# One table for the order of every engine's single steps, in block-causal attention followed by a gated MLP

## The chip, the core and the metric

The kernel runs on one core of one Trainium2 chip. The core has five engines with a queue of instructions each: TensorE (PE, matrix products into PSUM), VectorE (DVE), ScalarE (ACT), GpSimd (POOL) and SyncE (SP, which here only issues DMA transfers). Every engine works through its own queue in order, and engines wait for each other by semaphores. The metric is the device time of one execution in microseconds (us); three runs of the kernel before gave 657.11, 653.99 and 655.95, a median of 655.95.

## What is computed

Eight batches of eight heads, 576 positions, head size 64. The attention's output is the input of a gated MLP with a spatial mix. All inputs are float32.

```python
def _attn_ref(q, k, v):
    block = 64
    scores = scale * np.matmul(q, k.transpose(0, 1, 3, 2))
    mask = block_i >= block_j
    scores = np.where(mask, scores, -1000000000.0)
    scores = scores - np.max(scores, axis=-1, keepdims=True)
    attn = np.exp(scores)
    attn = attn / (np.sum(attn, axis=-1, keepdims=True) + 1e-09)
    return np.matmul(attn, v).astype(np.float32)

def _moe_ref(x, w_in, w_spatial, b_spatial, w_out):
    h = np.maximum(x @ w_in, 0.0)
    u, v = (h[..., :d_ff // 2], h[..., d_ff // 2:])
    v_n = (v - mu) / np.sqrt(var + 1e-06)
    v_s = np.einsum('ts,bsd->btd', w_spatial, v_n) + b_spatial[None, :, None]
    gated = u * v_s
    return (gated @ w_out).astype(np.float32)
```

Here x is the attention's output with the heads side by side (576 x 512), w_in is 512 x 1024, w_spatial 576 x 576, w_out 512 x 512; mu and var are the mean and variance of v over its 512 columns.

## The kernel before

**Attention.** Two heads are worked on together, a *pair*; a batch has four pairs, the program 32, counted here from 0. For a pair the scores of the five blocks of query rows (4 of 128 rows, one of 64, which the names call 8) go to PSUM banks of 512 float32 (`s`, line 619, and line 462 for the 64 rows). DVE masks them, takes their row maximum and moves them out in one instruction, a *top* (L434), ACT takes the exponential with its row sum (L441), DVE makes reciprocals of the sums (L528, L529), POOL multiplies by them (L532). The result P must be turned round before it can be multiplied by v. In the pairs of the first batch PE does that with a unit matrix (L299) and the copies L309 to L326; from pair 4 on DVE turns blocks of 32 x 32 (L674, L665), and SP regroups them by DMA (`ptt<-pb`, L686, L694). Then PE forms the weighted sums (`av`, L711, L723; L370 to L395 in the first batch), and ACT and DVE split them in two fp32r words (`x`, L345, L347). PSUM has 3 banks with the tag s, 2 with t, 1 with av, 2 with m.

**MLP.** All products take two or three fp32r passes: hi·hi, hi·lo, lo·hi. For a batch: five groups `mv` (v columns, by block of positions, L759; the last block of 64 positions, L770), eight `mu` (L838), eight `ms` (the spatial mix, L868 to L873), eight `mo` (the output, L894). All of them take the two m banks in turn, so group n+2 can start only when group n has been read out: `mv` and `mu` by ACT (L764, L843; `mv_4` also by DVE, L778), `ms` by DVE, which multiplies u in place (L875), `mo` by ACT. ACT copies an output group into a tile `o` (L900) and issues its store on its own DMA queue (L901). The pool of `o` has **two** buffers; the copy of a third tile waits until the store that reads one of them has landed. The names end in z, which of two halves of 288 positions, and in the group's number: `o_1_2` is z = 1, group 2.

**Order.** The tile framework works out the semaphores. The order on each engine is the order in which the Python program issues its instructions: `in_order()` ties every instruction to the one before it on its engine. That order was written by hand. The first stage works through 20 *sets* (pairs 0 to 4, five row blocks in four sets each) in one loop, with the decoding and splitting of the weights planned by step numbers (the tables `WEIGHTS` and `SPATIAL`). Then one loop goes through pairs 4 to 31, and works off the scores of the pair, the weighted sums of the pair before it and the MLP groups of the batch before it. A group `f` issues its products, `follow()` later issues what reads them out, in whole parts: a part of `out_group` is the products, the copy and the store together.

```python
            o = o_p.tile([P, HT], F32, tag="o", name=f"o_{b}_{z}_{ec}")
            nc.scalar.copy(o, ps[:, :HT])
            nc.scalar.dma_start(outT[b, es, z * HT:(z + 1) * HT], o)
            yield
```

Of the kernel before, what the change touches and what calls it, by code (L numbers as in the profile page):

```python
# [17 lines left out]
P = 128  # L18
S = 576
# [26 lines left out]
WEIGHTS = [  # L46
# [3 lines left out]
]  # L50
SPATIAL = [(6, 17), (6, 18), (9, 27), (9, 29), (16, 20)]
# [3 lines left out]
def kernel(  # L55
# [78 lines left out]
    def decode(hi, lo, to):  # L134

        f = to
        if to.dtype == I32:
# [8 lines left out]
            if step >= 20:  # L146
# [52 lines left out]
    def split_tail():  # L199
        r = spatial.pop(FULL)  # L200
        rows, both = slice(0, 64), (slice(64, 65), slice(96, 97))
        nc.scalar.copy(ws_a, r[:, 0, :])
        for one in both:
            nc.scalar.copy(ws_b[one, :], r[one, 1, :])
        for x, f, hi in (
# [3 lines left out]
            nc.gpsimd.tensor_tensor(out=x, in0=f, in1=hi.bitcast(F32), op=ALU.subtract)  # L209

# [14 lines left out]
    def split_pair(b, pr):  # L225

        hi = ff_p.tile([P, 896], F32R, tag="rw", name=f"hi_{b}_{pr}")
        lo = lo_p.tile([P, 896], F32R, tag="lo", name=f"lo_{b}_{pr}")
# [981 lines left out]
```

## Time and profile before

| | us |
|---|---|
| runs (median) | 657.11, 653.99, 655.95 (655.95) |
| span of the profiled execution | 653.2 |
| PE busy | 641.7 (98%) |
| DVE busy | 472.7 (72%) |
| ACT busy | 408.3 (63%) |
| POOL busy | 342.7 (52%) |
| first matmul of the span starts at | 1.05 |

The profile is of one execution, and the span, from its first recorded instruction to its last, is the only time that was kept of it; it lies 2.75 us below the median and 0.8 us below the fastest of the three runs. A working of times below is made against the span and carried over to the median. Busy time of PE is modelled from pipelined matmuls, so 98% says that it hardly ever waited, not that each matmul is as short as it can be.

### The profile page before, as it was taken

Reading aid. Unit: us, or ns where it says so; the run is one execution under the profiler, and the core shown is the slowest. Engines: PE = TensorE matmul, PEld = TensorE weight load, DVE = VectorE, ACT = ScalarE, POOL = GpSimd, SP = SyncE. Lnnn points to the kernel's source line nnn. Section 1 sums busy time; section 2 is a strip of 40 time slices with the busy share of each in tenths; the row PEclk is TensorE's granted clock in tenths of the full one; section 3 lists DMA queues with packets and bytes.
Section 4 is the critical chain, followed back from the end, with each engine's and each line's share of the span. In section 5 each row is a group of like instructions: output and inputs, shape, how many; then the busy total and the mean of one; then the engine's idle time right before and its main releaser. Section 6 shows DMA issues by size and latency. Waiting matters only on the chain.

```text
span 653.2 us, 15856 instructions
## 1 busy us (share of the span) xinstructions
PE 641.7 (98%) x5472; PEld 560.7 (86%) x5472; DVE 472.7 (72%) x1787; ACT 408.3 (63%) x1166; POOL 342.7 (52%) x566
## 2 busy tenths in 40 slices
PE   9999999999999999999999999999999999999998
PEld 5556777988999889998899889998899988998997
DVE  6889887878876787687786788766876868741420
ACT  5988975557855576556864578555765558632622
POOL 4868976634755346653564446552475535630130
PEclk9999999999999999999999999999999999999999
DMA  7544776775466755656566654667546564561002
GB/s 245 190 150 145 200 186 146 207 170 136 110 172 160 188 123 125 177 141 162 138 159 158 161 129 121 169 164 192 124 105 173 155 171 103 123 137 37 1 0 74
DMA packets 51109, 93.48 MB, mean 143 GB/s; under 512 B 5970, under 2 KB 27986, under 8 KB 51028
## 3 DMA queue, kind: packets, MB, share of 16 engines
q1 hardware_dynamic: 41812, 83.03, 50.4%
q10 hardware_dynamic: 9216, 9.44, 4.3%
q8 instruction: 43, 0.70, 0.4%
q14 instruction: 38, 0.31, 0.1%
HBM read 37.13 MB, written 9.44 MB: 71 GB/s over the span
## 4 chain that ended last, share of the span: by engine, by line
PE 79%; DVE 10%; ACT 3%; POOL 2%; DMA 2%; issue 1%; SPq 1%; DVEq 0%; POOLq 0%; ACTq 0%
PE mo L894 15%; PE mu L838 14%; PE ms L868 14%; PE mv L759 12%; PE av L711 8%; PE s L619 6%; DVE p L434 3%; PE s L462 2%; PE av L723 2%; PE mv L770 2%; DVE pb L674 1%; ACT p L441 1%; DMA ptt<-pb 1%; PE ms L873 1%; PE ms L872 1%
## 5 line engine op out<-in xcount | busy, mean ns | idle before, releaser
L532 POOL TENSOR_SCALAR p<-p,sst 128x256 f32<-128x256 f32 (+4 forms) x244 | 128.4, 543 | 73.8 <-DVE sst L529 60.3
L441 ACT ACTIVATE p<-p,sst 128x256 f32<-128x256 f32 (+4 forms) x244 | 134.7, 553 | 19.0 <-DVE sst L434 17.2
L838 PE MATMUL mu<-x,wi_hi 128*128 128x288 f32 x512 | 108.9, 296 | 1.4 <-DVE vr L778 1.4
L434 DVE CUSTOM_DVE_ANT_0 p<-s,mask 128x512 f32<-128x512 f32 (+1 forms) x216 | 92.6, 485 | 7.3 <-PE s L619 6.5
L674 DVE STREAM_TRANSPOSE pb<-p 128x512 f32<-128x512 f32 (+1 forms) x224 | 94.9, 473 | 0.5 <-POOL p L532 0.4
L838 PEld LDWEIGHTS mu<-x,wi_hi 128*128 128x128 f32 x512 | 84.1, 188 | 6.0 <-ACT p L441 2.2
L759 PE MATMUL mv<-wi_hi,x 128*128 128x512 f32 x256 | 85.7, 396 | 0.6 <-ACT x L345 0.6
L879 POOL TENSOR_TENSOR gl<-u,gh 128x288 fp32r<-128x288 f32 x59 | 47.2, 810 | 72.1 <-ACT gh L878 71.8
L818 POOL TENSOR_TENSOR vl<-vr,vh 128x512 fp32r<-128x512 f32 x32 | 41.3, 1290 | 74.9 <-ACT vh L817 74.0
L868 PE MATMUL ms<-ws_hi,vh 128*128 128x288 f32 x256 | 76.0, 297 | 0.4 <-DVE u L875 0.4
L868 PE MATMUL ms<-ws_hi,vl 128*128 128x288 f32 x256 | 75.7, 296 | 0.0
L868 PE MATMUL ms<-ws_lo,vh 128*128 128x288 f32 x256 | 75.4, 295 | 0.0
L711 PE MATMUL av<-ptt,v 128*64 128x64 f32 (+3 forms) x896 | 69.1, 304 | 2.2 <-DVE sst L434 0.9
L838 PE MATMUL mu<-x,wi_lo 128*128 128x288 f32 x256 | 69.8, 295 | 0.0
L711 PEld LDWEIGHTS av<-ptt,v 128*64 128x64 f32 x896 | 54.0, 137 | 16.9 <-DVE sst L434 2.7
L875 DVE TENSOR_TENSOR u<-ms,u 128x288 f32<-128x288 f32 x64 | 29.2, 456 | 53.5 <-PE ms L873 52.8
L759 PEld LDWEIGHTS mv<-wi_hi,x 128*128 128x128 f32 x256 | 48.0, 188 | 14.0 <-ACT p L441 2.6
L900 ACT COPY o<-mo 128x288 f32<-128x288 f32 x64 | 25.5, 398 | 51.6 <-PE mo L894 51.6
L878 ACT CAST gh<-u 128x288 fp32r<-128x288 f32 x60 | 24.3, 429 | 52.9 <-DVE u L875 52.9
L502 ACT ACTIVATE p<-p,sst 128x288 f32<-128x288 f32 x56 | 29.6, 528 | 43.9 <-DVE sst L487 37.5
L894 PE MATMUL mo<-gh,wo_hi 128*128 128x288 f32 x240 | 53.3, 303 | 0.2 <-ACT gh L878 0.2
L894 PE MATMUL mo<-gl,wo_hi 128*128 128x288 f32 x240 | 51.7, 296 | 0.2 <-POOL gl L879 0.2
(166 smaller groups left out, 1556.4 us busy)
## 6 DMA issues: line engine op xcount, KB each, us to landing
ptt<-pb SPq DMA_DIRECT2D x112, 320.0 KB, 6.0
raw<-qk SPq DMA_DIRECT2D x31, 576.0 KB, 4.1
v<-v SPq DMA_DIRECT2D x32, 320.0 KB, 5.4
outT<-o ACTq DMA_DIRECT2D x64, 144.0 KB, 4.0
ptt<-pb SPq DMA_DIRECT2D x112, 80.0 KB, 2.2
r_gh<-w_in SPq DMA_DIRECT2D x3, 512.0 KB, 3.6
r_gl<-w_in SPq DMA_DIRECT2D x3, 512.0 KB, 3.5
rs<-w_spT SPq DMA_DIRECT2D x4, 288.0 KB, 4.3
```

The lines of the kernel that those rows point to most:

```text
L434: nc.vector.tensor_tensor_reduce(out=p[:, at:at + n], in0=ps, in1=mk, scale=-0.125, scalar=BIG if m == 0 else st[:, k:k + 1], op0=ALU.add, ...
L441: nc.scalar.activation(p, p, AF.Exp, bias=mx, scale=-1.0, accum_out=st[:, 10 + k:11 + k])
L532: nc.gpsimd.tensor_scalar(out=p, in0=p, scalar1=st[:, k:k + 1], scalar2=1.0, op0=ALU.mult, op1=ALU.mult)
L619: mm(ps[(t, hd)], q[js, Q_AT[t]:Q_AT[t] + P], k[js, K0:K0 + n], start=(m == 0), stop=(m == len(of) - 1),)
L674: nc.vector.transpose(to(C_AT[hd][0] + 32 * t, dims), p)
L711: mm(to[js, :, 32 * c:], vt[:, c, js], ptt[:, 2 * z:2 * z + 2, at:at + P - 32 * c], start=(c == 0), stop=(c == 3),)
L759: mm(ps, xs[k][:, j, cs], w[:, k, DH:], start=(n == 0), stop=(n == 3 * NC - 1),)
L818: nc.gpsimd.tensor_tensor(out=vl, in0=vr, in1=vh.bitcast(F32), op=ALU.subtract)
L838: mm(ps[:, :HT], w[:, k, ds], xs[k][:, j, zs], start=(n == 0), stop=(n == 3 * NC - 1),)
L868: mm(ps[:, :HT], a[:, ds], w[:, k, zs], start=(n == 0), stop=False)
L879: (nc.vector if dc == ND - 1 and b == B - 1 else nc.gpsimd).tensor_tensor(out=gl[:, dc, :], in0=uz, in1=gh[:, dc, :].bitcast(F32), op=ALU. ...
L894: mm(ps[:, :HT], w[:, k, es], a[:, k, :], start=(n == 0), stop=(n == 3 * ND - 1),)
```

## The change

The work is the same: every engine has the same number of instructions of the same kinds and shapes. What changes is who says in which order they come. All functions that issue work become generators which yield after every single instruction or group of matmuls, and one string, `ORDER`, names the generator to be advanced next, from the first load to the last store. A word `o.5.1.2*2` advances output group 2 of half 1 of batch 5 by two steps; `step()` advances until at least one instruction has been issued.

```diff
+ORDER = """
+load.0 set.0*9 set.1*4 set.2 ns.0 set.2 ns.0*3 set.1 ns.1 ns.0 set.3*2 load.1 set.4*2 set.2*2
...
+n.28 t.28 n.28 t.28*2 a.27 n.28 o.5.1.0 o.5.1.1*2 r8.28 o.5.1.2 t.28 o.5.1.0 o.5.1.2*2 a.27
+o.5.1.3*2 r.28 v.6.0 loadv.29 8.29*4 v.6.0 v.6.4 v.6.0 8.29*3 v.6.0 v.6.4*3 u.6.0.0*2 s.29*6
...
-    def bank(nm):
-        pool, tag = RING[turn[0] % len(RING)]
-        turn[0] += 1
+    def bank(nm, k, b, pr):
+        pool, tag = RING[(10 * (b * NPAIR + pr) + k) % len(RING)]
         return pool.tile([P, 512], F32, tag=tag, name=nm)
...
+            yield
             o = o_p.tile([P, HT], F32, tag="o", name=f"o_{b}_{z}_{ec}")
             nc.scalar.copy(o, ps[:, :HT])
+            yield
             nc.scalar.dma_start(outT[b, es, z * HT:(z + 1) * HT], o)
             yield
...
+    def step(*key):
+
+        if key not in steps:
+            steps[key] = make[key[0]](*key[1:])
+        n = len(traced.instructions)
+        while len(traced.instructions) == n:
+            next(steps[key], None)
+        in_order()
+
+    for word in ORDER.split():
+        name, _, times = word.partition("*")
+        kind, *numbers = name.split(".")
+        for _ in range(int(times or 1)):
+            step(kind, *map(int, numbers))
```

PE's order is another one in the first 180 us or so (sets, MLP of batch 0, start of batch 1), then the same to the end but for two pairs of groups that change places in batch 6. The order on DVE, ACT, POOL and SP is another one in the first 200 us and from the output of batch 5 on (about 513 us), and the same between. Bank turns, which before followed the calls, now follow the pair's number.

Three places are shown. In the rows, an arrow stands between what is written and what is read, the last number of a name counts tiles through the program, and `[waits ...]` names the semaphores: of an engine, or DMAHW with a number for a transfer.

PE in the MLP of batch 0, about 72 to 76 us of the trace before. Before, `s_1_1`, the scores of pair 5 (batch 1, pair 1), follow the last products of `mv_4`:

```order
L770 MATMUL mv_4_1021<-wi_hi,xs_255 128x512
L770 MATMUL mv_4_1021<-wi_lo,xs_255 128x512
L619 MATMUL s_1_1_0_1040<-raw_1_665 128x512
L619 MATMUL s_1_1_1_1042<-raw_1_665 128x512
L619 MATMUL s_1_1_0_1044<-raw_1_665 128x384
L619 MATMUL s_1_1_1_1046<-raw_1_665 128x384
L619 MATMUL s_1_1_0_1048<-raw_1_665 128x256
L619 MATMUL s_1_1_1_1050<-raw_1_665 128x256
L619 MATMUL s_1_1_0_1048<-raw_1_665 128x128
L619 MATMUL s_1_1_1_1050<-raw_1_665 128x128
```

In the change:

```order
L755 MATMUL s_1_1_0_906<-raw_1_615 128x512
L755 MATMUL s_1_1_1_908<-raw_1_615 128x512
L755 MATMUL s_1_1_0_910<-raw_1_615 128x384
L755 MATMUL s_1_1_1_912<-raw_1_615 128x384
L755 MATMUL s_1_1_0_914<-raw_1_615 128x256
L755 MATMUL s_1_1_1_916<-raw_1_615 128x256
L755 MATMUL s_1_1_0_914<-raw_1_615 128x128
L755 MATMUL s_1_1_1_916<-raw_1_615 128x128
L982 MATMUL mu_1_0_943<-x_0_300,wi_hi 128x288
L982 MATMUL mu_1_0_943<-x_0_300,wi_lo 128x288
L982 MATMUL mu_1_0_943<-x_1_507,wi_hi 128x288
```

The scores of pair 5 have moved ahead of two `mu` groups, `mv_3` and `mv_4`, which followed them at once or later; `mu_0_1`, the group that needs the bank of `mv_4`, still comes after the weighted sums of pair 4, as before.

DVE at the same place. Before, the tops of pair 5 end, its P is turned, and the addition that reads out `mv_4` (L778) follows after three blocks:

```order
L434 ISA p_1_1_1_1075,sst_1_966<-s_1_1_1_1050,mask 128x128
L434 ISA sst_1_966 128x1
L528 TENSOR_SCALAR sst_1_966<-sst_1_966 128x6
L529 RECIPROCAL sst_1_966<-sst_1_966 128x2
L665 STREAM_TRANSPOSE pb_1_1084<-p_99 128x5x2x32 x2
L674 STREAM_TRANSPOSE pb_1_1084<-p_1_1_0_1054 128x4x4x32
L528 TENSOR_SCALAR sst_1_966<-sst_1_966 128x12
L529 RECIPROCAL sst_1_966<-sst_1_966 128x4
L674 STREAM_TRANSPOSE pb_1_1084<-p_1_1_1_1057 128x4x4x32
L778 TENSOR_TENSOR vr_4_1022<-mv_4_1021,vr_4_1022 64x512
L674 STREAM_TRANSPOSE pb_1_1084<-p_1_1_0_1060 128x3x4x32
```

In the change:

```order
L652 TENSOR_SCALAR sst_1_775<-sst_1_775 128x6
L653 RECIPROCAL sst_1_775<-sst_1_775 128x2
L552 ISA p_1_1_1_1057,sst_1_775<-s_1_1_1_916,mask 128x128
L552 ISA sst_1_775 128x1
L927 BN_STATS st_3_982<-vr_3_981 128x6
L928 BN_AGGR st_3_982<-st_3_982 128x2
L262 SCALAR_TENSOR_TENSOR r_rw<-r_rw 128x512
L793 STREAM_TRANSPOSE pb_1_1071<-p_99 128x5x2x32
L918 TENSOR_TENSOR vr_4_1030<-mv_4_1029,vr_4_1030 64x512
L793 STREAM_TRANSPOSE pb_1_1071<-p_99 128x5x2x32
```

The addition (now L918) stands behind the tops as it did, but these tops read scores that PE has formed four groups earlier, and only one turned block is ahead of it.

ACT at the output of batch 5, half 1 (about 516 to 524 us of the trace before), `o_1_0` to `o_1_3`. Before:

```order
L345 CAST x_3_7458<-av_3_0_7449 128x256 [waits PE_49]
L345 CAST x_3_7458<-av_3_1_7461 128x320 [waits PE_49]
L900 COPY o_1_0_7512<-mo_1_0_7499 128x288 [waits DMAHW3_49,PE_49]
L901 DMA outT<-o_1_0_7512 128x288 [waits Activation_49]
L230 CAST hi_1_7520<-raw_1_7204 128x896 [waits Pool_49]
L900 COPY o_1_1_7538<-mo_1_1_7525 128x288 [waits DMAHW5_49,PE_49]
L901 DMA outT<-o_1_1_7538 128x288 [waits Activation_49]
L900 COPY o_1_2_7558<-mo_1_2_7545 128x288 [waits DMAHW3_49,PE_49]
L901 DMA outT<-o_1_2_7558 128x288 [waits DMAHW0_49,Activation_49]
L900 COPY o_1_3_7574<-mo_1_3_7561 128x288 [waits DMAHW5_49,PE_49]
L901 DMA outT<-o_1_3_7574 128x288 [waits Activation_49]
L502 ACTIVATE p_99,sst_1_7481<-p_99,sst_1_7481 128x288 [waits DVE_49]
```

In the change:

```order
L560 ACTIVATE p_7_0_0_7432,sst_0_7196<-p_7_0_0_7432,sst_0_7196 128x128 [waits DVE_49]
L560 ACTIVATE p_7_0_1_7442,sst_0_7196<-p_7_0_1_7442,sst_0_7196 128x256 [waits DVE_49]
L461 CAST x_3_7448<-av_3_0_7419 128x256 [waits PE_49]
L560 ACTIVATE p_7_0_1_7442,sst_0_7196<-p_7_0_1_7442,sst_0_7196 128x128 [waits DVE_49]
L461 CAST x_3_7448<-av_3_1_7450 128x320 [waits PE_49]
L1046 COPY o_1_0_7516<-mo_1_0_7496 128x288 [waits DMAHW3_49,PE_49]
L1046 COPY o_1_1_7531<-mo_1_1_7518 128x288 [waits DMAHW5_49,PE_49]
L1048 DMA outT<-o_1_0_7516 128x288 [waits Activation_49]
L1046 COPY o_1_2_7553<-mo_1_2_7538 128x288 [waits DMAHW3_49,PE_49]
L1048 DMA outT<-o_1_2_7553 128x288 [waits DMAHW7_49,Activation_49]
L1046 COPY o_1_3_7570<-mo_1_3_7557 128x288 [waits DMAHW7_49,PE_49]
L623 ACTIVATE p_99,sst_1_7478<-p_99,sst_1_7478 128x288 [waits DVE_49]
```

Before, each copy is followed by its own store, and a copy waits for the store of two copies earlier. In the change the store of `o_1_0` comes after the copy of `o_1_1`, the copy of `o_1_2` waits for that store (DMAHW3), and the copy of `o_1_3` for the store of `o_1_2` (DMAHW7), which stands right ahead of it; the store of `o_1_1` comes ten instructions after that last copy. The cast `hi_1` has moved ahead of the last exponentials. Something like it stands at the output of batch 0: there `o_0_1` is stored seven instructions after its copy, and the copies of `o_0_0`, `o_1_2` and `o_1_0` each wait for a store issued shortly ahead of them.

## Rows read from the trace of the kernel before

**Rows 1.** The page, part 1: busy time, share, instructions.
```profile
PE 641.7 (98%) x5472; PEld 560.7 (86%) x5472; DVE 472.7 (72%) x1787; ACT 408.3 (63%) x1166; POOL 342.7 (52%) x566
```

**Rows 2.** The page, part 4: the chain by engine.
```profile
PE 79%; DVE 10%; ACT 3%; POOL 2%; DMA 2%; issue 1%; SPq 1%; DVEq 0%; POOLq 0%; ACTq 0%
```

**Rows 3.** Windows: us, busy per engine (instructions), granted clock, DMA share, GB/s.
```profile
0.00:56.00 56.00, 52.60 (x346) 31.28 (x347) 44.30 (x178) 44.39 (x130) 36.72 (x66) 1.00 0.60 200
56.00:112.00 56.00, 52.26 (x398) 42.80 (x398) 46.75 (x171) 41.49 (x112) 47.32 (x69) 1.00 0.62 157
112.00:580.00 468.00, 467.38 (x4225) 420.54 (x4222) 364.34 (x1390) 297.46 (x866) 245.22 (x417) 1.00 0.60 150
580.00:653.20 73.20, 69.47 (x509) 66.07 (x507) 17.33 (x50) 24.99 (x59) 13.45 (x15) 1.00 0.16 45
```

**Rows 4.** Timeline of PE, 30 to 60 us: start, duration, instruction [idle before <-releaser].
```profile
33.05 0.87 PE L370 MATMUL av<-ptlo,v 128*64 128x256 f32 x8 [0.66 <-DVE sst L528]
...
58.50 0.50 PE L759 MATMUL mv<-wi_hi,x 128*128 128x512 f32 x1 [0.64 <-ACT x L345]
```

**Rows 5.** Timeline of PE, 73 to 97 us.
```profile
75.86 2.40 PE L711 MATMUL av<-ptt,v 128*64 128x256 f32 x32
78.09 0.75 PE L723 MATMUL av<-ptt,v 128*64 128x64 f32 x20
...
81.98 0.37 PE L838 MATMUL mu<-x,wi_hi 128*128 128x288 f32 x1 [1.36 <-DVE vr L778]
...
93.93 1.31 PE L711 MATMUL av<-ptt,v 128*64 128x256 f32 x16 [0.55 <-DVE sst L434]
95.59 1.31 PE L711 MATMUL av<-ptt,v 128*64 128x256 f32 x16 [0.35 <-DVE sst L434]
```

**Rows 6.** Timeline of DVE, 73 to 84 us.
```profile
74.66 0.69 DVE L434 CUSTOM_DVE_ANT_0 p<-s,mask 128x512 f32<-128x512 f32 x1 [0.20 <-PE s L619]
...
81.19 0.65 DVE L778 TENSOR_TENSOR vr<-mv,vr 64x512 f32<-64x512 f32 x1
```

**Rows 7.** Timeline of ACT, 509 to 532 us.
```profile
518.30 0.34 ACTq L901 DMA_DIRECT2D outT<-o  x1
518.68 0.94 ACT L230 CAST hi<-raw 128x896 fp32r<-128x896 f32 x1 [0.41 <-POOL p L532]
519.53 0.39 ACT L900 COPY o<-mo 128x288 f32<-128x288 f32 x1
...
521.06 0.40 ACT L900 COPY o<-mo 128x288 f32<-128x288 f32 x1 [1.14 <-PE mo L894]
521.49 0.37 ACTq L901 DMA_DIRECT2D outT<-o  x1
522.66 0.40 ACT L900 COPY o<-mo 128x288 f32<-128x288 f32 x1 [1.20 <-PE mo L894]
```

**Rows 8.** Timeline of PE, 515 to 532 us.
```profile
522.46 0.40 PE L759 MATMUL mv<-wi_hi,x 128*128 128x512 f32 x1
...
525.21 0.39 PE L770 MATMUL mv<-wi_hi,xs 128*128 128x512 f32 x1
...
527.07 0.30 PE L838 MATMUL mu<-x,wi_hi 128*128 128x288 f32 x1
...
528.74 0.50 PE L619 MATMUL s<-hi 64*128 64x512 f32 x2
```

**Rows 9.** Timeline of SP, 509 to 532 us.
```profile
520.70 5.73 SPq L694 DMA_DIRECT2D ptt<-pb  x4
```

**Rows 10.** Tile outT, 515 to 525 us: its four stores, from issue to landing.
```profile
DMA to landing us min/median/max: 2.4/5.9/6.4
```

**Rows 11.** Tile outT, 590 to 598 us: its four stores.
```profile
DMA to landing us min/median/max: 1.7/1.8/1.8
```

**Rows 12.** Tile outT, 130 to 142 us: its four stores.
```profile
DMA to landing us min/median/max: 2.4/6.1/6.2
```

**Rows 13.** Timeline of PE, 580 to 653 us.
```profile
588.35 1.31 PE L711 MATMUL av<-ptt,v 128*64 128x256 f32 x16 [0.66 <-DMA ptt<-pb]
```

More of the change, by code (lines that the diff above doesn't have):

```diff
@@ L162, in decode, with split @@
             yield
-        split(hi, lo, f)
+        yield from split(hi, lo, f, k >= 6)
         yield
-    def split(hi, lo, f):
-        if step >= 20:
+    def split(hi, lo, f, late=False):
+        if late:
             nc.gpsimd.tensor_scalar(
@@ L404, in av_hi @@
             next(e)
+            yield
         yield
         for e in evacs:
-            run(e)
+            next(e, None)
+            yield
         yield
@@ L505, in top_8 @@
             )
-        return [(8, hd, ns[hd]) for hd in range(2)]
+            yield
     def norm_8(st):
@@ L563, in scores_set @@
             for z in range(2):
-                ps = next(banks)
+                ps = s_bank(2 * which + z)
                 for hd in range(2):
@@ L574, in scores_set @@
             yield
-            top(st, 8, 0, p[:, :S], parts)
-            yield [(8, 0, p[:, :S])]
+            yield from top(st, 8, 0, p[:, :S], parts)
+            tiles_of[which] = [(8, 0, p[:, :S])]
+            yield
             return
-        ps = [next(banks) for hd in range(2)]
+        ps = [s_bank(2 * which + hd) for hd in range(2)]
         at = {t: sum(P * (x + 1) for x in ts if x > t) for t in ts}
@@ L731, in av_pair @@
         for e in evacs:
-            run(e)
+            next(e, None)
+            yield
         tail_evac(b, pr)
@@ L737, in moe @@
     def moe(b):
-        xs = [xts.pop((b, pr)) for pr in range(NPAIR)]
-        xs_tail = tails.pop(b)
+        xs = [x_tiles(b, pr) for pr in range(NPAIR)]
+        xs_tail = tail_tile(b)
         vn = {}
@@ L1064 @@
-    for e in evac:
-        run(e)
-    norm(stats[pairs[NPAIR]], tiles_of[19])
-    behind = []
-    def follow():
-        for e in behind[::-1] if step >= 28 else list(behind):
-            if next(e, e) is e:
-                behind.remove(e)
-    def issue(f, last=False):
-        gen = f()
-        if not last and step < 28:
-            follow()
-        next(gen)
-        if not last and step >= 28:
-            follow()
-        behind.append(gen)
-        next_step()
-    SPLIT = (1, 2, 2, 2)
@@ L1148, with norm_set, turn_set, once @@
-    run(av_pair(*pairs[-1]))
-    for f in rest + sum(moe(B - 1), []):
-        issue(f)
-    for e in behind:
-        run(e)
+    def norm_set(n):
+        if sets[n][0] == NPAIR:
+            for t, hd, p in tiles_of[n]:
+                p_of[(*pairs[NPAIR], t, hd)] = p
+        yield from norm(sst(*pairs[sets[n][0]]), tiles_of[n])
+    def turn_set(n):
+        yield from transposes(*pairs[sets[n][0]], tiles_of[n], 2 * n)
+    def once(f, *args):
+        f(*args)
+        yield
+    def turns(g):
+        b, pr = pairs[g]
+        for t, hd in ((3, 0), (3, 1), (2, 0), (1, 0), (0, 0), (2, 1), (1, 1), (0, 1)):
+            yield from turn_blocks(b, pr, t, hd)
@@ new lines, in pad_8, with group @@
+    def pad_8():
+        nc.gpsimd.memset(p8.rearrange("p (h k) -> p h k", h=2)[:, :, HT:], 0.0)
+    mlps = {}
+    def group(kind, b, *k):
+        if b not in mlps:
+            mlps[b] = moe(b)
+        yield from mlps[b](kind, *k)
+    make = {
+        "load": lambda g: once(load_pair, *pairs[g]), "loadv": lambda g: once(load_v, *pairs[g]),
+        "w": weight, "sw": spatial_w, "set": scores_set, "ns": norm_set, "ts": turn_set,
+        "alo": lambda g: av_lo(*pairs[g]), "ahi": lambda g: av_hi(*pairs[g]),
+        "pad": lambda: once(pad_8),
+        "s": lambda g: scores_run(*pairs[g]), "n": lambda g: norms(*pairs[g]), "t": turns,
+        "8": lambda g: scores_8(*pairs[g]), "t8": lambda g: turn_blocks(*pairs[g], 8, 0),
+        "a": lambda g: av_pair(*pairs[g]), "split": lambda g: split_pair(*pairs[g]),
+        "r8": lambda g: once(regroup_8, *pairs[g]), "r": lambda g: once(regroup, *pairs[g]),
+        "v": lambda b, *k: group("v", b, *k), "u": lambda b, *k: group("u", b, *k),
+        "g": lambda b, *k: group("g", b, *k), "o": lambda b, *k: group("o", b, *k),
+    }
```

469 lines of the change are left out of this document (226 added, 243 removed), and 3 rows, old and new, of the table WEIGHTS.

## The prediction, made before the changed kernel had run

> **What bounds the kernel now.** I read the page first, then the chain, then the time axis cut in stages, then the single waits. PE is busy for 641.7 of 653.2 us [rows 1], and the chain that ended last runs over PE for 79% of the span [rows 2]: whatever keeps PE from its next product lengthens the run, and nothing else does. The stages say where it is kept [rows 3]. From 0 to 56 us (the sets) PE stands for 56 − 52.60 = 3.40 us, of which 1.05 lie ahead of the first product. From 56 to 112 us (MLP of batch 0 beside the first pairs of batch 1) it stands for 3.74 us. Then, for 468 us, for 0.62 in all. After 580 us it stands for 3.73: 0.66 before the last pair's weighted sums [rows 13], the rest behind the last product, while the last output is copied and stored. So at most 2.35 + 3.74 + 0.62 + 0.66 = 7.4 us can be won by a better order, 1.1% of the time: no product is removed or shortened, the granted clock is at its full level in each of these stages [rows 3], and the stretch behind the last product keeps its order. On the other hand a table that only closes these gaps must open none, and a single new wait of some us eats them up.
>
> **Sets, 0 to 56 us.** Each engine's order is new here. The waits of before go, the longest being 0.66 at 33.05 [rows 4], where PE's first weighted sums waited for DVE. In their place some score groups ask for a bank earlier than its top is done, and the transposes queue behind them on PE. Followed by hand with the durations of the trace, four such places give waits of one or two tops each, a top of 512 columns being 0.69 us [rows 6]. The bounds: half to most of the 2.35 us won, or four places of two tops (5.5 us) less the 2.35 won and less what DVE's earlier work gives back, some 1.5 us lost. I take **+0.2** (−1.6 to +1.5), since the tops that move earlier and those that come late are of one size.
>
> **MLP of batch 0, 56 to 112 us.** Three waits of before have a clear cause that the new order removes.
> - At 58.50 the last quarter of `mv_0` waited 0.64 us for the cast of x, behind the exponentials on ACT [rows 4]. In the change more scores stand between the weighted sums and `mv_0`: 0.64 won.
> - At 81.98 `mu_1_1` waited 1.36 us for DVE to read `mv_4` out (L778) [rows 5]. The addition ran at 81.19, behind tops that began at 74.66, right behind their scores [rows 6]. The change forms these scores four groups earlier, so that DVE is through with the tops when `mv_4` ends; behind `mv_4` PE also has 3.1 us of weighted sums (75.86 and 78.09 [rows 5]) before a group needs that bank. 1.36 won.
> - At 93.93 and 95.59 pair 5's weighted sums waited 0.55 and 0.35 us for banks that tops held [rows 5]. In the change two `mu` and two `ms` groups go between: 0.90 won.
>
> Against these 2.90 stand new short waits (`ms_0_1` now comes first and needs the last split of v; a score bank waits for a cast of x): 0.4, after the smaller of the gaps shown. DVE is busy for 46.75 of these 56 us [rows 3], so PE cannot run far ahead of it. I take **−2.5** (−3.6, nearly all idle time gone, to −0.5, if DVE binds).
>
> **Output of batch 0.** The copies of `o_0_0`, `o_1_2` and `o_1_0` wait for stores that were issued shortly ahead. Four stores near 135 us landed after 2.4 to 6.2 us [rows 12]. For `o_1_2`: a copy of 0.40, the cast hi of 0.94 [rows 7], a landing of 2.4, a copy of 0.40, in all 4.1 us after `mo_1_1`, while PE has the weighted sums of 3.1 us and a few scores before it needs the bank: 0.7 late. With a landing of 6.2 it would be 3.8 more. The regroup of pair 8 has not started by then, so I take **+0.7** (0 to +4.5); the other two have more work before them.
>
> **Output of batch 5, the term that decides.** Here the order of ACT changes in a stretch where PE before had no gap. The two m banks hold `mo_1_2` and `mo_1_3` until they are copied; `mv_0` and `mv_4` of batch 6 need these banks, at 522.46 and 525.21 [rows 8]. Before, copies ran at 519.53, 521.06 and 522.66, each as its products ended [rows 7]: the store it waited for had been issued nearly 3 us earlier. In the change:
> - `hi` (0.94) and the exponentials move ahead, so the copy of `o_1_1` starts when its products end, about 519.5, and ends at 519.9. Only now the store of `o_1_0` goes out.
> - It lands after 2.4 us, the least of [rows 10], where the store of 518.30 [rows 7] is the one issued well ahead of the regroup; the copy of `o_1_2` runs from 522.3 to 522.7: `mv_0` starts 0.25 late.
> - Its store goes out at 522.7. SP's regroup of pair 28 (four transfers of L694) before began at 520.70 and took 5.73 us to issue [rows 9]; in the change, with the last exponentials about 1 us later, it begins at about 521.6. Before, the store of 521.49 and the one behind the copy of 522.66 [rows 7] were issued 0.8 and 2.4 us into it, and the median and the longest landing of the four stores are 5.9 and 6.4 us [rows 10]. With 6.2 the store lands at 528.9.
> - The copy of `o_1_3` ends at 529.3, and only then `mv_4` can start: 529.3 − 525.21 = 4.1 us late, the 0.25 within. Nothing on PE can go round it: `mv_4` is next in its queue. The 288-column exponentials and the read-out of `mv_0`, queued behind that copy on ACT, take less than `mv_4` itself (527.07 − 525.21 = 1.86 [rows 8]), so the stop is not paid twice.
>
> I take **+4.1**. The low end is a store that lands in 2.4 us: the copy ends at 525.5, 0.3 late. The high end is that both stores meet the regroup, 5.9 us each: 519.9 + 5.9 + 0.4 + 5.9 + 0.4 = 532.5, 7.3 late. The case between lies nearest to rows, since stores in this phase have 5.9 and more as a rule: the median of the four is 5.9 here and 6.1 near 135 us [rows 10, 12].
>
> **Output of batch 6, and the end.** The same kind of order stands at 592 us, but no regroup is left by then and stores land in 1.8 us [rows 11]: a chain of two landings delays a copy by 1.4 us, while the banks leave 2.75 us (`mv_0`, 525.21 − 522.46 [rows 8]). Nothing. The wait of 0.66 at 588.35 for the last regroup [rows 13] shrinks, as DVE's turning of pair 31 starts a little earlier: **−0.3** (−0.66 to 0). All other moves after 180 us lie on engines that PE does not wait for [rows 3].
>
> **Sum:** 0.2 − 2.5 + 0.7 + 4.1 − 0.3 = +2.2 us. The profiled span would go from 653.2 to 655.4; it lies 2.75 us below the median of the runs, and against the median, 655.95, the same +2.2 gives **658.2 us**. A measurement of this kernel tells a difference from none at about 0.5%, 3.3 us: below 652.7 it is faster, above 659.2 slower. The forecast is inside, on the slow side.
>
> **Rivals.**
> 1. *The store does not wait for the regroup.* The store has 128 x 288 x 4 bytes, the regroup's four transfers hold a pair's whole P, many times that; if the store's packets pass between the regroup's, it lands early and the term of 4.1 becomes 0.3: −1.6, 654.4 us. For it: one of the four landed in 2.4 us. Against it: only the first two were issued before the regroup began, and the median of the four is 5.9 [rows 10]. The Trainium skill, "DMA: Bandwidth & Descriptors", section "Queues, rings and completion order", says that each DMA engine takes turns between the queues, a packet at a time; by that rule a small store should be far ahead of the regroup, and the rows near 520 us do not agree.
> 2. *The gaps close as well.* With rival 1 and the good ends of the first stages (−1.6 and −3.6, no loss at batch 0's output, −0.5 at the end) the change gives −5.4: 650.5 us. For it: every gap lies where the order is new. Against it: DVE's load in those 56 us.
> 3. *Slower: the stop at `mv_4` costs PE its clock.* The stop of 4 us would be six times the longest gap that the trace shows past 100 us, and all stages have the full level of 2.4 GHz. Should the granted clock fall to 1.2 GHz there, `mv_4` and `mu_0_0` would take twice their 1.86 and 1.67 us (to 528.74): 3.5 more, 661.7 us. It is decided by the stop's length, and no row here shows a longer one. The Trainium skill, "TensorE: Matmul & The Clock Gate", Part 1, has the clock fall back after a stretch of idleness; no run here shows that yet.
>
> **How the numbers follow.** Forecast (stop at `mv_4`, full clock) 0.55: its first-stage terms are uncertain by some 2 us, which puts 0.15 of it above 659.2 and 0.02 below 652.7. Rival 1 alone 0.18, a third of it below 652.7. Rival 2 0.12. Rival 3 0.15. Faster 0.02 + 0.06 + 0.12 = 0.20; slower 0.15 + 0.15 = 0.30; no difference 0.50. The range goes from between rivals 1 and 2 to rival 3, 651.5 to 661.8; what it leaves out is about half of rival 2, nearly half of rival 3 and a little of the forecast's tail.
>
> **What would show it.** In the changed profile: PE with a wait of about 4 us before the `mv` of the last 64 positions near 525 us, given to ACT's copy of `o`, and that copy waiting for `outT`; no wait above 0.5 us before the `mu` near 80 us and before the weighted sums near 94; idle time from 0 to 56 us as before within 1.5 us, from 56 to 112 us near 1.2. Wrong it is if that wait is missing or under 1 us, if stores issued into a regroup land within 3 us, or if the first 112 us are shorter by over 4 us, or longer.

## The result, and the profile after

The changed kernel takes **646.02 us** (median of 4 runs, 645.55 to 646.93), the kernel before in the same rounds 655.01: a ratio of 0.9861 (0.9838 to 0.9884), 9 us or 1.4% faster. The prediction said 658.2 and slower; the time lies under its range. A second series of the changed kernel gave 645.95. The profiled execution took 646.17 us, with a span of 644.4.

From the page of the changed kernel (span; part 1; the granted clock; the chain by engine):

```profile
span 644.4 us, 15835 instructions
PE 636.3 (99%) x5472; PEld 559.9 (87%) x5472; DVE 473.1 (73%) x1787; ACT 408.6 (63%) x1166; POOL 341.2 (53%) x566
PEclk9999999999999999999999999999999999999999
PE 93%; DVE 2%; POOL 2%; ACT 2%; DMA 1%; issue 0%; SPq 0%; POOLq 0%
```

PE does the same 5472 instructions at the same clock, and yet its *busy* time fell from 641.7 [rows 1] to 636.3: 5.4 of the 8.8 us that the span lost; the other 3.4 were idle. The chain runs over PE for 93%, before for 79% [rows 2]. The stages (windows, columns as in [rows 3]):

```profile
0.00:56.00 56.00, 52.92 (x370) 33.74 (x371) 46.40 (x183) 46.77 (x135) 37.23 (x68) 1.00 0.57 192
56.00:112.00 56.00, 55.03 (x471) 46.82 (x470) 51.57 (x199) 45.90 (x130) 48.96 (x72) 1.00 0.71 192
```

In the first 56 us PE is idle for 3.08 us, before for 3.40 [rows 3], but gets through 370 records instead of 346. Cut where PE reaches the first `mv` of batch 0 and of batch 6 (same columns; first the kernel before, then the changed one):

```profile
0.00:55.53 55.53, 52.13 (x345) 30.86 (x345) 44.17 (x177) 43.92 (x128) 36.25 (x66) 1.00 0.60 200
55.53:522.46 466.93, 462.68 (x4120) 412.18 (x4119) 367.42 (x1396) 301.55 (x870) 263.87 (x436) 1.00 0.61 154
522.46:653.24 130.78, 126.90 (x1012) 117.65 (x1010) 61.15 (x217) 62.86 (x169) 42.59 (x66) 1.00 0.32 81
```
```profile
0.00:51.91 51.91, 48.83 (x352) 30.34 (x353) 42.59 (x169) 44.01 (x127) 33.14 (x61) 1.00 0.56 188
51.91:514.61 462.70, 460.80 (x4113) 412.01 (x4111) 368.43 (x1399) 301.08 (x872) 266.04 (x440) 1.00 0.63 158
514.61:644.39 129.78, 126.63 (x1012) 117.53 (x1010) 62.10 (x221) 63.55 (x169) 42.01 (x66) 1.00 0.32 83
```

Up to the first `mv` PE saves 0.3 us of idle time and 3.3 of busy time, with eight more score records done (the 345 count the `mv` that begins there); from there to batch 6 2.35 of idle and 1.9 of busy time. The longest things that PE waited for in the whole run (engine, line, releaser: us in total, times, longest):

```profile
PE s_first L717 <- DMA raw<-qk: 1.2, 1, 1.2
PE warm L208 <- DVE mask L202: 1.1, 1, 1.1
PE mu L982 <- ACT vr L904: 1.0, 1, 1.0
```

How a wait hides in busy time is seen at one place. PE's timeline, first of the kernel before, then of the changed one, at the same eight score records (four of 256 columns and four of 128, half of each for either head; the row names the first form only):

```profile
17.06 0.70 PE L584 MATMUL s_first<-raw 64*128 64x256 f32 x2
17.96 0.92 PE L584 MATMUL s_first<-raw 64*128 64x256 f32 x6 [0.20 <-DVE sst L434]
```
```profile
15.36 0.92 PE L717 MATMUL s_first<-raw 64*128 64x256 f32 x8
```

Two records, a wait for a bank, six records: 17.06 to 18.88, 1.82 us, of which 0.20 is shown as idle. Without the wait the eight take 0.92. So 0.9 was lost and 0.2 shown. The same timelines in narrow windows (17.06 to 17.30 before, 15.44 to 15.60 in the changed kernel) say where the rest went:

```profile
17.06 0.48 PE L584 MATMUL s_first<-raw 64*128 64x256 f32 x1
```
```profile
15.36 0.49 PE L717 MATMUL s_first<-raw 64*128 64x256 f32 x2
```

In the changed kernel the products of two heads, of 64 rows each, run side by side: two take 0.49 us. Before, one runs alone in 0.48; the next product in PE's program, the other head's, starts only when its bank is free, at 17.96, 0.9 us after the first. For 0.7 of that time the first head's two records keep PE busy, and only the rest is booked as idle. Records also overlap the next ones: in the same stretch transposes of 128 columns last 0.27 us each and start every 0.11, so that a wait of under 0.16 leaves no gap. This is one place; how the 5.4 us divide between such places is not shown.

When PE reaches the first `mv` of batch 0 and of batch 6 (PE's timeline), and the span of the profiled execution; h_sets, h_mlp and h_first are the hybrids of the next section, t_before has the order before and a_again the changed one once more:

| | mv_0, batch 0 | mv_0, batch 6 | span | median |
|---|---|---|---|---|
| before | 55.53 | 522.46 | 653.2 | 655.0 |
| h_sets | 51.67 | 520.11 | 650.8 | 653.65 |
| h_mlp | 55.59 | 517.97 | 649.3 | 650.95 |
| h_first | 52.10 | 515.41 | 645.2 | 645.9 |
| after | 51.91 | 514.61 | 644.4 | 646.0 |
| t_before | 56.17 | 523.15 | 653.0 | 654.3 |
| a_again | 51.44 | 514.31 | 644.2 | 645.95 |

The lead over before is 3.6 us at the first `mv`, 7.85 at batch 6, 8.8 at the end. By t_before and a_again, such a position differs by 0.3 to 0.7 us from one profile of the same order to the next.

### The profile page after: what moved, and what is told of

Same layout as the page of the kernel before. It is cut to its first block, busy times and chain, and to the rows that moved or that the text cites. A ratio compares the mean times of both kernels' runs of the same rounds, so it can differ in the third digit from the quotient of the medians.

```text
span 644.4 us, 15835 instructions
## 1 busy us (share of the span) xinstructions
PE 636.3 (99%) x5472; PEld 559.9 (87%) x5472; DVE 473.1 (73%) x1787; ACT 408.6 (63%) x1166; POOL 341.2 (53%) x566
## 4 chain that ended last, share of the span: by engine, by line
PE 93%; DVE 2%; POOL 2%; ACT 2%; DMA 1%; issue 0%; SPq 0%; POOLq 0%
PE mo L1039 16%; PE ms L1013 16%; PE mu L982 16%; PE mv L898 13%; PE av L848 9%; PE s L755 7%; PE s L581 3%; PE av L860 3%; PE mv L910 2%; PE s_first L717 2%; PE t L408 2%; PE ms L1018 1%; PE ms L1017 1%; DVE p L552 1%; POOL wi_lo L281 1%; DMA raw<-qk 1%
## 5 line engine op out<-in xcount | busy, mean ns | idle before, releaser
L657 POOL TENSOR_SCALAR p<-p,sst 128x512 f32<-128x512 f32 (+4 forms) x244 | 128.8, 547 | 61.0 <-DVE sst L653 52.3
L560 ACT ACTIVATE p<-p,sst 128x256 f32<-128x256 f32 (+3 forms) x244 | 135.0, 555 | 19.5 <-DVE sst L552 18.7
L1039 PE MATMUL mo<-gh,wo_lo 128*128 128x288 f32 x240 | 51.5, 296 | 0.0
```

The costliest lines, as they stand in the source:

```text
L560: nc.scalar.activation(p, p, AF.Exp, bias=mx, scale=-1.0, accum_out=st[:, 10 + k:11 + k])
L657: nc.gpsimd.tensor_scalar(out=p, in0=p, scalar1=st[:, k:k + 1], scalar2=1.0, op0=ALU.mult, op1=ALU.mult)
L1039: mm(ps[:, :HT], w[:, k, es], a[:, k, :], start=(n == 0), stop=(n == 3 * ND - 1),)
```

## The experiments

All tables use the changed program; their words are those of `ORDER`. A step is one advance of a generator, numbered by its place in the changed table. Medians are set against before in the same rounds (654.8).

| kernel | us | ratio to before |
|---|---|---|
| t_before | 654.34 | 0.9988 (0.9977 to 0.9999) |
| h_sets | 653.65 | 0.9982 (0.9971 to 0.9993) |
| h_mlp | 650.95 | 0.9933 (0.9919 to 0.9947) |
| h_first | 645.9 | 0.9856 (0.9839 to 0.9873) |
| x_late | 659.29 | 1.0056 (1.0041 to 1.0072) |
| x_hi | 649.62 | 0.9914 (0.9894 to 0.9934) |
| x_dec | 648.13 | 0.9901 (0.9872 to 0.9931) |
| h_late | 648.91 | 0.991 (0.9895 to 0.9924) |
| mix_sp | 671.0 | 1.0247 (1.0222 to 1.0273) |
| x_cast | 647.4 | 0.9883 (0.9868 to 0.9898) |
| h_sw | 654.65 | 1.0003 (0.9993 to 1.0014) |
| m_vadd | 654.92 | 1.0 (0.9989 to 1.001) |
| m_vs | 656.49 | 1.0018 (1.0008 to 1.0028) |
| m_two | 654.46 | 0.9993 (0.9984 to 1.0002) |
| m_pe | 654.14 | 0.9988 (0.9974 to 1.0002) |
| x_best | 646.44 | 0.9869 (0.9853 to 0.9886) |
| a_again (after) | 645.95 | 0.9861 (0.9844 to 0.9878) |

### Which stretch of the order gains

```diff
 t_before: the order before
 h_sets:   the order before
+          with the new order for steps 0 to 346 (to the first mv)
 h_mlp:    the order before
+          with the new order from the first mv to step 1013 (first output of batch 1)
 h_first:  the order before
+          with the new order for steps 0 to 1013
```

> The changed program with a table that gives every engine the kernel before's own order, instruction by instruction. Theory A (the gain is in the order of the first 113 us and the last 60): 655.0 us, within 0.3% of before. Rival B (the step-by-step code itself gains, by other buffers and semaphores with the same order): near 646, and no part of the order would be worth anything.

> The new order only up to the first v matmul of batch 0 (the start and the score sets), the order before from there on. Theory A: 650.5 us (4.5 us less than before: what the first v matmul of the changed kernel leads by), with PE's busy time lower by about 3 us and its idle time by about 1. The prediction's step for this stretch (its idle waits only swap places): 655.2, at best 653.4.

> The order before up to the first v matmul of batch 0, the new order for the MLP of batch 0 and the start of batch 1, the order before from there on. Theory A: 651.9 us (3.9 less for the MLP, 0.8 more for the start of batch 1). The prediction's terms: 2.5 less and 0.7 more, 653.2. If the lead in the MLP is only a consequence of the earlier sets: 655.

> The new order up to the first output of batch 1 (sets, MLP of batch 0, start of batch 1), the order before from there to the end. Theory A: 647.4 us (7.6 less), the sum of the two parts alone; the rest of the 9 us is the end. If the parts are not independent, the sum of the two alone differs from it by over 1 us.

The program alone, with its new turns of the banks, gives 0.1%. The first 1014 steps give all of the gain; h_first and after differ by 0.1 us, so the new end is worth nothing that these runs show. But the parts do not add up: 1.2 alone and 3.9 alone, 8.9 together. h_sets reaches the first `mv` as early as the changed kernel and loses the lead within 15 us. ACT's and PE's timelines of h_sets, and the window behind:

```profile
59.40 0.67 ACT L292 CAST ws_a<-rt 128x576 fp32r<-128x576 f32 x1 [2.02 <-DMA rt<-w_spT]
60.10 1.36 ACT L295 CAST ws_b<-rt 1x576 fp32r<-1x576 f32 x2
61.48 0.60 ACT L889 ACTIVATE vr<-mv 128x512 f32<-128x512 f32 x1
```
```profile
62.13 0.40 PE L967 MATMUL mu<-x,wi_hi 128*128 128x288 f32 x1 [1.97 <-ACT vr L889]
...
63.33 0.45 PE L967 MATMUL mu<-x,wi_hi 128*128 128x288 f32 x1
```
```profile
62.00:66.00 4.00, 3.87 (x18) 3.87 (x19) 3.72 (x12) 3.52 (x10) 3.75 (x5) 0.58 0.84 137
```

PE came earlier, the load of the last spatial weights did not: ACT waits 2.02 us for it, with the bank of a finished `mv` unread behind it in its queue. PE stops for 1.97 us, and then the granted clock is 0.58 in the mean (1.00 before the stop): `mu` products come every 0.24 us instead of 0.13. The 19 products from 62.13 to 66.15 have 18 steps, 4.02 us instead of 18 x 0.132 = 2.4, so the stop costs another 1.6. In the new order these casts stand behind other work of ACT.

### The output of batch 5

x_late is the stores of the prediction's deciding step alone, in the order before, with the cast of `hi` left between the copies; x_hi undoes one move in the changed kernel, that cast and its two subtractions.

```diff
 x_late
 o.5.1.0*2
-o.5.1.0
...
 o.5.1.1*2
-o.5.1.1
 r.28 o.5.1.2
+o.5.1.0
 o.5.1.2*2
-o.5.1.3
...
 x_hi
-split.29
...
 n.28 o.5.1.0
+split.29
 o.5.1.1*2
...
 o.5.1.2 t.28
+split.29*2
 o.5.1.0 o.5.1.2
```

> The kernel before's order with only the four stores of the output of batch 5 moved to where the change has them (store of o_1_0 behind the copy of o_1_1, store of o_1_1 and o_1_3 much later); the cast to hi stays between the copies. This is the step of the prediction by itself: 4.1 us more, 659, with PE stopped before mv_4. Rival (the stop does not come): 655.0 and no stop.

> The changed kernel with one move undone at the output of batch 5: the cast to hi of pair 29 on ACT and the two subtractions to lo go back between the first two copies, as before. DVE's transposes of pair 28 then end about 0.6 us earlier, ACT's copies shift later, and the regroup on SP starts before the store of o_1_2 instead of 0.4 us after it. The prediction's step: that store takes 5.9 us instead of 1.8, the copy of o_1_3 comes 4 us later, and PE stops 2.5 to 4 us before mv_4: 648.5 to 650. Rival (the banks cover the copies in any case): 646.0, no stop over 0.5 us between 510 and 525 us.

x_late: 4.5 us slower than before. x_hi: 3.6 us slower than after. The step of the prediction was right as a mechanism, and the change escapes it by 0.4 us. The changed kernel (ACT's timeline, SP's, the landings from 506 to 522 us, PE's):

```profile
511.62 0.34 ACTq L1048 DMA_DIRECT2D outT<-o  x1
513.48 0.40 ACT L1046 COPY o<-mo 128x288 f32<-128x288 f32 x1 [1.46 <-DMA outT<-o]
513.91 0.34 ACTq L1048 DMA_DIRECT2D outT<-o  x1
515.75 0.40 ACT L1046 COPY o<-mo 128x288 f32<-128x288 f32 x1 [1.88 <-DMA outT<-o]
```
```profile
514.33 5.14 SPq L831 DMA_DIRECT2D ptt<-pb  x4
```
```profile
DMA to landing us min/median/max: 1.8/1.8/1.8
```
```profile
517.36 0.39 PE L910 MATMUL mv<-wi_hi,xs 128*128 128x512 f32 x1
```

The same in x_hi (ACT; SP; landing of the second store; PE; a window):

```profile
514.36 0.34 ACTq L1045 DMA_DIRECT2D outT<-o  x1
519.66 0.40 ACT L1043 COPY o<-mo 128x288 f32<-128x288 f32 x1 [5.33 <-DMA outT<-o]
```
```profile
513.55 5.44 SPq L828 DMA_DIRECT2D ptt<-pb  x4
```
```profile
DMA to landing us min/median/max: 5.2/5.2/5.2
```
```profile
520.11 0.50 PE L907 MATMUL mv<-wi_hi,xs 128*128 128x512 f32 x1 [2.21 <-ACT o L1043]
...
521.16 0.63 PE L907 MATMUL mv<-wi_lo,xs 128*128 128x512 f32 x1
```
```profile
521.00:523.00 2.00, 2.00 (x6) 1.54 (x6) 1.28 (x5) 0.99 (x5) 0.00 (x0) 0.50 0.84 252
```

A store issued 0.42 us ahead of the regroup lands in 1.8 us; issued 0.81 us into it, in 5.2. The DMA queues of x_hi behind that issue, from 514.4 to 516.5 us and from 516.5 to 519.3 (packets, MB, share of 16 engines; q10 carries ACT's stores, q1 SP's transfers):

```profile
q1 hardware_dynamic: 81, 0.21, 76.2%
```
```profile
q1 hardware_dynamic: 225, 0.51, 84.0%
q10 hardware_dynamic: 144, 0.15, 16.2%
```

None of the store's 144 packets runs in the first 2.1 us, then all of them run among the regroup's. PE stops for 2.21 us and goes on at half clock: from the start of `mv_4` to the first score behind `mu_0_0` it takes 520.11 to 525.30, 5.19 us, in the changed kernel 517.36 to 520.89, 3.53. In x_late the stop is 2.75 us and the clock behind it (PE; window):

```profile
528.03 0.78 PE L893 MATMUL mv<-wi_hi,xs 128*128 128x512 f32 x1 [2.75 <-ACT o L1029]
```
```profile
528.00:532.00 4.00, 3.97 (x12) 3.25 (x13) 0.79 (x5) 1.75 (x6) 0.99 (x2) 0.57 0.57 154
```

That is 4 x (1 - 0.57) = 1.7 us: 2.75 + 1.7 = 4.45, and 4.5 between the medians. In the profiled run PE is 4.4 us behind at the next `mv` (538.76 against 534.33) and 3.6 at the end. Of the seven runs of x_late the two with a mean granted clock of 1.0 take 656.71 and 657.05, the five with 0.997 take 658.65 to 659.52: the clock makes about half of the price, and does not fall each time.

### Where the start gains

x_dec puts the first decoding steps on DVE ahead of the score reads again; h_late uses the order before for the first 28 us; mix_sp keeps the new order on all engines but SP.

```diff
 x_dec
 set.2
+w.0*2
 set.3 ts.0*4
+w.0
 set.3 ns.1 ns.2
+w.0
 set.5
+w.1*2
 set.5*2
+w.1
 set.5
+w.1
 set.5
...
 h_late
+the order before for its first 150 steps, then the new order
...
 mix_sp, SP's loads in the order
-load.1 w.0 w.1 loadv.0 w.2 load.2 loadv.1 sw.0 w.3 load.3 w.4 load.4 sw.1
+load.1 loadv.0 w.0 loadv.1 w.1 w.2 load.2 w.3 w.4 sw.0 sw.1 load.3 loadv.2 w.5
...
```

> The changed kernel with one part of the start undone: DVE's first four decoding steps of the weights (two of each of two blocks, 2.8 us in all) and their two ACT steps stand ahead of the reads of the score banks of pair 1 again, as before. Theory (the sets' lead comes from the score banks being read before the weights are decoded): PE falls back by 1 to 2.5 us up to the first v matmul, most of it inside what the profile calls busy, and the time is 647 to 648.5. Rival (the lead comes from the order of PE's own transposes and scores): within 0.5 of 646.0.

> The order before for the first 150 steps of the table (up to about 28 us), the new order from there to the end. It tells where in the start the lead arises. Theory (score banks read ahead of the weights' decoding, most of it in the first 20 us, as x_dec says): 2.0 to 2.5 above the changed kernel, 648.0 to 648.5. If the lead were spread evenly over the 52 us before the first v matmul: 648.1 as well; if it arises behind 28 us: 646.5.

> The changed kernel with only SP's queue of loads in the order before, up to the first v matmul; all other engines in the new order. If the new order of the loads carries a part of the lead at the start (what x_dec does not explain, about 1.8 us): 647 to 648. If the loads come in time either way: 646.0.

x_dec is 2.1 us above after and reaches the first `mv` at 53.59, 1.68 later; its four runs spread from 646.46 to 651.08 and its interval just meets that of after, so the trace carries this more than the time. PE's timeline in x_dec, then in the changed kernel:

```profile
12.69 0.91 PE L714 MATMUL s_first<-raw 64*128 64x384 f32 x2
14.23 0.91 PE L714 MATMUL s_first<-raw 64*128 64x384 f32 x2 [0.64 <-DVE sst L549]
```
```profile
12.93 1.15 PE L717 MATMUL s_first<-raw 64*128 64x384 f32 x4
```

12.69 to 15.14 against 12.93 to 14.08: 1.3 us lost, 0.64 of it shown; again one head's products run alone first. h_late is 2.9 above after and reaches the first `mv` at 54.58: 2.7 of the lead of 3.6 arise in the first 28 us. mix_sp missed every expectation: 25 us above after. Its PE waits and SP's timeline, and a window:

```profile
PE s L578 <- DMA raw<-qk: 8.1, 1, 8.1
PE s_first L578 <- DMA raw<-qk: 5.4, 1, 5.4
PE av L501 <- ACT pthi L436: 3.3, 1, 3.3
```
```profile
47.64 0.38 SPq L370 DMA_DIRECT2D v<-v  x1
65.88 0.38 SPq L232 DMA_DIRECT2D r_gl<-w_in  x1
66.35 0.46 SPq L325 DMA_DIRECT2D raw<-qk  x1
```
```profile
66.00:76.00 10.00, 4.93 (x27) 2.90 (x28) 1.93 (x8) 0.66 (x3) 2.60 (x5) 0.53 0.59 195
```

The weights' load `r_gl` waits on SP until 65.88 for its buffer (POOL's last read of the block before begins at 65.1 and takes 0.74), since the new order decodes late, and the load of a pair's `raw` stands behind it; PE waits 8.1 us for that. So decoding late pays only because the change moves the loads in SP's queue with it.

### The MLP of batch 0, stop by stop

```diff
 x_cast (from after)
 v.0.0*2
+sw.4*3
...
-sw.4*3
 sw.4 8.5*2
...
 h_sw (from h_sets)
 v.0.0*2
-sw.4*5
...
 v.0.2*2
+sw.4*5
...
 m_vadd (from t_before)
 s.5 n.5
+v.0.4
...
 a.4 v.0.3
-v.0.4
...
 m_vs (from t_before; m_two is m_vadd with m_vs)
 v.0.4
-v.0.4*3
 w.10*2
...
-w.10
 u.0.1.3*2
-w.10*3
...
 8.6 s.6
+v.0.4*3 w.10*4
...
 m_pe (from m_two)
 8.6*2
+s.6
 u.0.0.3*2
...
 load.7
-s.6
...
 x_best (from after)
 v.0.1 w.7
+v.0.1
...
 8.5*2
-v.0.1
...
+s.10*3
 v.1.3*3
-s.10*3
```

> The changed kernel with one part undone: ACT's three casts of the last rows of the spatial weights and their bias stand behind the first read of a v bank again, as before, ahead of the reads of the two next v banks. The part alone at h_sets cost a stop of 1.97 us on PE, because ACT waited 2.02 us there for the weights' DMA with the v banks unread behind it. Theory (the sets' lead is lost if that cast is met early): ACT waits about 1.5 us for the DMA at 58 to 59 us, PE's stop before the u matmul at 65 grows from 0.97 to 2.5 us, and the time is 647.6 us. Rival (the lead was lost in h_sets by its order as a whole): 646.0, no longer stop.

> The order of h_sets (new up to the first v matmul, then as before) with ACT's three casts of the last spatial weights, and POOL's two steps that need them, behind the reads of the first three v banks. Theory (h_sets gained only 1.2 us because those casts, met 3.9 us earlier, waited 2.02 us for their DMA in front of the v banks): PE's stop of 1.97 us before the first u matmul falls under 0.4, and the time is about 651.7, 2 us below h_sets. Rival (what holds h_sets back is the wait for DVE's addition at 80 us, or the weights' DMA elsewhere): still 653 to 653.7.

> The kernel before's order with one step moved: DVE's addition that frees the bank of mv_4 of batch 0 stands in front of the four transposes and the two small steps ahead of it (2.5 us). The prediction took 1.36 us for this step, the stop of PE before the u matmul at 82 us: 653.4. Theory of waits hidden in busy time: at least that, 653.4 or up to 0.3 less. Rival (another wait ends as late): 654.8.

> The kernel before's order with one group moved in the MLP of batch 0: DVE's last two steps of mv_4 (cast to vs_b, subtraction to vs_a) and one decoding of an output weight, with the ACT and POOL steps behind them, stand behind the first two reads of the score banks of pair 6 instead of ahead (3.0 us of DVE's work and a wait of 0.88 us for ACT). Theory (from 82 to 96 us of the kernel before DVE's queue sets PE's pace): the stops of 0.55 and 0.35 us before the av matmuls at 94 and 96 close, 0.9 less, 653.9. Rival (a stop closed alone always comes back, as in m_vadd): 654.8.

> m_vadd and m_vs together: the addition earlier, and the three DVE steps behind the reads of pair 6. Theory (the stop that m_vadd closed at 82 us came back at 94 because DVE read the scores of pair 6 no earlier; with both, PE keeps it): 1.36 and 0.9 less, 652.5, more than the sum of the two alone. Rival (DVE is full over the whole MLP, and the stop comes back at the ms or mo groups): 654 to 654.8.

> m_two with one piece of PE's order moved as well: the score matmuls of pair 6 (2.4 us) stand in front of the last two u groups of batch 0 (24 matmuls, 3.2 us), as in the new order, so that PE has work while DVE reads the scores. In m_two the stop before the av matmuls at 93 us was 1.19 us. Theory (the gain of the new order in the MLP needs both: DVE's order, and matmuls between a pair's scores and its av): that stop closes, 653.2, 1.5 to 1.8 below before, though m_vadd gave nothing, m_vs lost and m_two gave 0.4. Rival (the stop moves on to the ms groups): 654.4.

> The changed kernel with its two later stops of PE taken on: ACT reads the bank of mv_1 of batch 0 in front of the casts of the last spatial weights (stop of 0.97 us at 65 us), and the statistics of mv_3 of batch 1 on DVE, with the steps behind them, stand behind the first two reads of the score banks of pair 10 (stop of 0.52 at 162 us). If both stops close: 644.6, 1.4 below the changed kernel. If the next wait on ACT or on the weights' DMA ends as late: 645.5 to 646.

> The changed kernel itself once more, in the same rounds: 646.0, and beside h_first (645.9, the order before at the end) it says that the new end is worth under 0.5 us. The prediction's step for the end: 0.3 less than with the old end; the trace's lead from 590 us on: 0.9 to 1.0.

**m_vadd** closes the stop of 1.36 us at 82 us [rows 5] and gains nothing. PE's timeline:

```profile
93.65 1.31 PE L830 MATMUL av<-ptt,v 128*64 128x256 f32 x16 [1.53 <-DVE sst L534]
```

The stop of 0.55 at 93.93 [rows 5] has become 1.53: PE came earlier, DVE's reads of pair 6 only 0.28 us earlier (92.91 against 93.19 on DVE's timeline). **m_vs** brings those reads forward and makes `ms` wait for DVE instead, and the clock falls behind that stop (PE; window):

```profile
102.13 0.40 PE L995 MATMUL ms<-ws_hi,vh 128*128 128x288 f32 x1 [1.74 <-DVE u L1003]
```
```profile
102.00:106.00 4.00, 3.87 (x20) 3.87 (x21) 3.79 (x11) 2.02 (x4) 2.38 (x5) 0.68 0.48 84
```

**m_two** still stops, since its scores stand right ahead of the `av`; **m_pe** puts 24 `mu` products between, as the new order does, and meets the regroup next (m_two, then m_pe):

```profile
93.01 1.31 PE L830 MATMUL av<-ptt,v 128*64 128x256 f32 x16 [1.19 <-DVE sst L534]
```
```profile
94.44 1.31 PE L830 MATMUL av<-ptt,v 128*64 128x256 f32 x16 [0.99 <-DMA ptt<-pb]
```

In m_pe's profile, of a run of 653.11, PE reaches batch 6 at 520.71, 1.75 us ahead of before; its 12 runs spread from 652.38 to 656.03, and their median is only 0.6 below before's, not clear of zero. So the theory behind m_pe is seen in the trace and not shown in time. **h_sw** does not test what it was meant to: ACT's third read stands behind the statistics that wait for DVE (4.26 us), and PE stops at 63.63, 67.61 and 82.07 for 1.67, 2.12 and 2.08 us. **x_cast**: the stop grows from 0.97 to 1.53 us, not to 2.5, and the interval overlaps that of after. **x_best** closes both stops and is no faster: in batch 0 PE is at `mv_4` 0.68 us earlier than in after and at the first `mo` 0.48 later, little more than two profiles of one order differ by. Within these runs the changed kernel remains the best.

## Why the prediction was wrong

- **The bound of 7.4 us.** It summed PE's idle time, and 98% busy was read as PE hardly ever waiting. The span lost 8.8, because 5.4 lay in busy time. The prediction's own signs for idle time came true, 3.08 us against 3.40 up to 56 us and 0.97 behind it where 1.2 had been named, while PE got to batch 6 7.85 us sooner. The Trainium skill, "Perfetto Trace Analysis", section "Identifying the Most-Contended Engine", says that the busy share of matmuls is no good measure of how close a kernel is to its roofline, since pipelined instructions look smaller in the trace. The 641.7 and 636.3 us for the same 5472 instructions agree that it is no good measure, though here the time looks larger, by the waits in it. This is the error that put the faster cases out of sight.
- **Sets, +0.2.** Measured -3.6 at the first `mv`. The working set four new waits against 2.35 us of shown idle time. It counted tops against tops and not what stood between them: DVE's decoding of weights (0.4 to 1.1 us a step), which the change moves behind the reads. Undoing four such steps puts PE back by 1.7 us there (x_dec); what gives the other half is not shown.
- **MLP of batch 0 and its output, -2.5 and +0.7.** In place of -1.8 the trace has -4.2 (7.85 less 3.6) and h_mlp -3.9. Sign and place were right, the size was not: idle time fell by 2.35 us, near the 2.5 that the working took for it, and 1.9 came out of busy time, with no stop at the output. The working priced each closed stop at its size, 1.36 for the one at 82 us; m_vadd shows that alone it is worth 0. That the stops close together is put down here to several queues changing their order at once, which is argued and, but for m_pe's profile, not shown. That the lead of the sets comes through is a product of this part too: h_sets loses most of it.
- **Output of batch 5, +4.1.** Measured 0 in the change, 4.5 in x_late. The mechanism, both copies waiting for stores (3.3 us in all), is there. What failed is the timing of the second store against the regroup: predicted 1.1 us into it, it went out 0.42 ahead. In the prediction the regroup began 1.1 us before `mv_0` and the store went out level with it; measured, the regroup begins 0.28 us before `mv_0` and the store goes out 0.70 before it. Three sizes make up these 1.5 us, about: the first store goes out as the copy ahead of it begins (both at 511.62), not as it ends, 0.4; it lands in 1.8 us where the working took 2.4, 0.6; and the regroup starts some 0.6 later than set. Undoing one cast and its two subtractions brings the stop back (x_hi). That x_late's 4.5 lies near the 4.1 is luck: its stop is 2.75 us, and the rest is the clock, which the forecast had at its full level. A term that hangs on which of two transfers is issued first, with half a microsecond between, had no right to 0.7 of the chance (the forecast and rival 3, against rivals 1 and 2).
- **End, -0.3.** The wait of 0.66 [rows 13] is gone in the changed kernel, but also in the profiles of t_before and h_first, which have the old order there: behind batch 6 PE and the output take 129.8 us in all three, 130.8 in before. So the new order did not earn it; h_first and after have the same median, and in time the end is 0 within some 0.5.
- **Rivals.** Rival 1 gave the right sign for this term for another reason: the store did not pass between the regroup's packets, it went ahead of them. The Trainium skill, "DMA: Bandwidth & Descriptors", section "Queues, rings and completion order", has each engine take turns between queues, a whole packet at a time. The packets of x_hi, which run side by side from 516.5 us, do not speak against that, but a small store is not early by it: 5.2 us against 1.8. Rival 2 named the outcome, with a time 4.5 too high. Rival 3's price is confirmed in kind: the clock fell to 0.50 behind the stop in x_hi; it cost 1.7 us where 3.5 had been set, since it came back earlier. That the stop's length decides it, as rival 3 has it, does not hold: see the last section.

Open: which of the new order's many moves in the MLP carry the 3.9 us. m_pe shows three of them doing part of it in the profile.

## What to carry to other kernels

Judge a pipelined engine by the start-to-start time of like groups, not by its idle time. Do not price a stop at its size: ask what the releasing engine does next, and whether the following wait on the same queue ends any earlier; two orders that fit each other (loads and decoding, scores and reads) gain together and lose alone. Where two transfers are issued within a microsecond of each other, work the case out for both orders and split the chance.

## What the runs showed of the hardware

- A stop of PE costs more than itself once the granted clock falls from 2.4 to 1.2 GHz behind it: seen behind stops of 1.74 (m_vs), 1.97 (h_sets), 2.08 (h_sw), 2.21 (x_hi) and 2.75 us (x_late), each costing about 1.5 to 1.7 us more, and behind those of 3.3, 5.4 and 8.1 us in mix_sp; not behind 1.53 (m_vadd, x_cast) and 1.61 (x_dec), nor behind 1.67 and 2.12 in h_sw. So length alone does not decide it; what does was not tried.
- One 144 KB store took 1.8 us to land ahead of a regroup and 5.2 beside it (x_hi; 5.7 in x_late, issued 1.16 us into it). In x_hi none of its packets ran in the first 2.1 us behind the issue.
- Score products of two heads, of 64 rows each, run side by side: two of 256 columns took 0.49 us, one alone 0.48.
- One load that waits for its buffer holds all loads behind it on SP's queue: 8.1 us of PE's time in mix_sp.
